# Two of three MLP squares moved to ScalarE, and a planner that keeps a margin ahead of TensorE's attention steps

## The chip, the core and the metric

The kernel runs on one core of one Trainium2 chip. The metric is the device time of one execution in microseconds (us). The median of three runs of the kernel before is 218.18 us (218.15 to 218.87).

## What is computed

Two layers follow each other. The first is a recurrent attention over 4 batches, 8 heads, 768 positions and a head size of 48:

```python
for t in range(S):
    cur = einsum('bhd,bhe->bhde', u[None] * kt, vt)
    y[:, :, t] = einsum('bhd,bhde->bhe', rt, state + cur)
    state = wt[..., None] * state + einsum('bhd,bhe->bhde', kt, vt)
```

The second is an MLP on the 3072 rows of `y` (384 wide, hidden 2048):

```python
h = x @ w_in
r = maximum(h, 0)
out = (s * (r * r) + b) @ w_out
```

## The kernel before, in words

The attention is cut into 24 chunks of 128 positions (6 along the sequence for each of 4 batches; chunk `n` is position block `n // 4` of batch `n % 4`). Within a chunk the recurrence is written as matrix products. A chunk passes these steps, each a small function:

- SyncE issues four loads of 192 KB: `w`, `r`, `k`, `v` (line 212).
- ScalarE takes the logarithm of `w` (`ln`, line 219). TensorE sums it along the chunk (`cum`, lines 268 to 276). ScalarE takes the exponential (`exp`, lines 290 and 294). VectorE multiplies `r` and `k` by it (`mul`, tile `prd`, line 300).
- TensorE transposes the result (`tr`, tile `trps`, line 327), ScalarE copies it out (`tev`, tile `RK`, line 342), TensorE multiplies keys and queries (`mt`, line 352), VectorE masks (`msk`, tile `mt_sb`, line 364), and TensorE forms `y` from the state and the masked scores (`ymm`, lines 380 and 389).
- VectorE adds a diagonal part (`yev`, tile `x_sb`, line 419). That part is made on GpSimd (`rkp`, `rku`, `yd`, lines 224, 235, 255) with a reduction on VectorE between (`cd`, line 249). TensorE transposes again (`xtr`, line 467) and ScalarE copies into the MLP's input `xT` (`xev`, line 482).
- The state is updated by TensorE (`dmm`, line 405), VectorE (`sup`, line 447) and GpSimd (`st`, line 456). `v` is cast to bf16 (`vb`), on GpSimd for the first 8 chunks (line 601) and on ScalarE for the other 16 (line 599), by the string `VBE`.

The MLP works on 12 tiles `T` of 256 rows (two chunks each). A tile has 8 pieces `g1` (6 matmuls of 256 columns each, line 516, into PSUM `h_ps`, 2 buffers). ScalarE applies the ReLU to each (`rh`, line 529) and VectorE squares it (`sq`, tile `gT`, line 534). Then come 8 pieces `g2` (4 matmuls of 384 columns each, line 549, into `o_ps`), four for each half tile, and VectorE scales and adds a constant (`oev`, tile `o_sb`, line 559). The store stands in the same SyncE queue as the loads. The two weights arrive in four pieces each and are cast to bf16: `CIE = 'APAP'` says that `w_in` is cast in turn by ScalarE (A) and GpSimd (P), and `COE = 'ADAD'` that `w_out` is cast by ScalarE and VectorE (D). A sum over `w_out` (`colsum`, line 578) and one ScalarE instruction (`bconst`, line 585) stand before the first `g2`.

The order of the instructions is not that of the loops. A class `Plan` holds each step with its engine, an assumed duration, the steps that it depends on, the buffers that it takes and a priority. It plays the steps through in time by these assumed numbers: again and again the step that can start first is put behind the others of its engine (ties go to the lower priority number). The steps are then written out in that order, and on the chip each engine takes its own in that order and waits where an operand is not there. Attention steps have low priority numbers, MLP pieces on TensorE high ones, so that these fill TensorE's gaps. Steps marked `port=True` (GpSimd's, `mul` and `sq` on VectorE) are planned one at a time.

Before the first 28 us of the plan are over, TensorE's planned gaps are filled with matmuls on a tile of zeros (`warm`, line 757), so many as fit into the gap at 0.125 us each.

Of the kernel before, what the change touches and what calls it, by code (L numbers as in the profile page):

```python
# [10 lines left out]
AF = mybir.ActivationFunctionType  # L11
ALU = mybir.AluOpType
# [4 lines left out]
WIN_AT = 35.0  # L17
WOUT_AT = 45.0
CIE = 'APAP'
COE = 'ADAD'  # L20
VBE = 'P' * 8 + 'A' * 16
WARM = 28.0


class Plan:
# [7 lines left out]
        self.ops = {}  # L33

    def add(self, name, eng, occ, fn, args=(), deps=(), takes=(), prio=0.0,
            lat=0.12, port=False, dma=0.0):
        self.ops[name] = dict(
            name=name, eng=eng, occ=occ, fn=fn, args=args, deps=list(deps),
            takes=list(takes), prio=prio, lat=lat, port=port, dma=dma,
            n=len(self.ops),  # L40
        )

    def order(self):
        ops = self.ops
        end = {}
        free = {}
        port = 0.0
        dma = 0.0
        held = {tag: [] for tag in self.rings}
        queues = {}  # L50
        for o in sorted(ops.values(), key=lambda o: (o["prio"], o["n"])):
            queues.setdefault(o["eng"], []).append(o)
        out = []

        def ready(o):
            t = 0.0
# [12 lines left out]

        while any(queues.values()):  # L70
            best = None
            for eng, q in queues.items():
                e = free.get(eng, 0.0)
                pick = None
                for o in q[: 1 if eng == "SP" else 400]:
                    r = ready(o)
                    if r is None:
# [9 lines left out]
            t, o = best  # L87
# [18 lines left out]
def kernel(  # L106
# [27 lines left out]
    FPQ = 512 // TOK  # L134
    NQ = FT // FPQ
# [104 lines left out]
    def castv(n):  # L240
        c = cb[n]
        vb = work.tile([128, H, D], BF16, name="vb", tag="vb", bufs=6)
        cast(VBE[n], vb, c["v"])
        c["vb"] = vb

    def cdiag(n):
# [280 lines left out]
    def relu(T, i):  # L527
        rh = mlp.tile([128, FPQ, TOK], BF16, name="rh", tag="rh", bufs=4)
        nc.scalar.activation(out=rh, in_=hs[T, i], func=AF.Relu)  # L529
        hs[T, i] = rh  # L530

    def square(T, i):
        rh = hs.pop((T, i))
        nc.vector.tensor_tensor(  # L534
            out=gT[T][:, i * FPQ : (i + 1) * FPQ, :], in0=rh, in1=rh, op=ALU.mult
        )

    os_ = {}

# [82 lines left out]
    for n in range(N):  # L622
        cc, bb = coords(n)
        T, j = divmod(n, CPT)
        keep = cc < NCH - 1
        P = 10.0 * n
        add(("ln", n), "ACT", 0.45, ln, (n,), [("load", n, 0)] + ([("ln", n - 1)] if n else []),
            [("lw", [("cum", n)])], P)
        add(("rkp", n), "POOL", 1.0, pool1, (n,), [("load", n, 1), ("load", n, 2)],
            [("rkp", [("rku", n)])], P, port=True)  # L630
        add(("rku", n), "POOL", 1.0, pool1b, (n,), [("rkp", n), "load_u"],
            [("rku", [("cd", n)])], P, port=True)
        e = CAST[VBE[n]][0]
# [7 lines left out]
        add(("cum", n), "PE", 0.45, cum, (n,), [("ln", n)],  # L641
            [("A", [("exp", n)])], P, lat=0.2)
# [6 lines left out]
        add(("tr", n), "PE", 0.44, trans, (n,), [("mul", n)],  # L649
            [("B", [("tev", n)]), ("RK", [("mt", n), ("ymm", n)])], P - 3, lat=0.2)  # L650
# [6 lines left out]
        add(("ymm", n), "PE", 0.37, ymm, (n,), [("msk", n), ("vb", n)] + prev  # L657
            + ([("sup", n)] if keep else [("supn", n)]),
            [("B", [("yev", n)]), ("x", [("xtr", n)])], P - 6, lat=0.2)
        add(("yev", n), "DVE", 0.48, yevac, (n,), [("ymm", n), ("yd", n)], [], P - 7)  # L660
        add(("xtr", n), "PE", 0.17, xtr, (n,), [("yev", n)],
            [("B", [("xev", n)])], P - 8, lat=0.2)
        add(("xev", n), "ACT", 0.4, xevac, (n,),
            [("xtr", n)] + ([("xev", n - 1)] if j else []),
            [("xT", [("g1", T, NQ - 1)])] if j == 0 else [], P - 8)
        if keep:
            add(("l2", n), "POOL", 0.17, lam2, (n,), [("exp", n)],
                [("l2", [("st", n)])], P - 2, port=True)
            add(("dmm", n), "PE", 0.16, dmm, (n,), [("mul", n), ("vb", n), ("l2", n)] + prev,
                [("B", [("sup", n)])], P - 4, lat=0.2)  # L670
            add(("sup", n), "DVE", 0.48, supd, (n,), [("dmm", n), ("l2", n)] + prev,
                [("stmp", [("st", n)])] if cc else [], P - 5)
            if cc:
                add(("st", n), "POOL", 0.8, sscale, (n,), [("sup", n), ("l2", n)]
                    + [("ymm", n - B)], [], P - 4, port=True)
            else:
                add(("st", n), "DVE", 0.0, lambda n: None, (n,), [("sup", n)], [], P - 5)
        else:
            add(("supn", n), "DVE", 0.0, supd, (n,), [("mul", n)] + prev, [], P - 5)

    BIG = 1000.0
    for T in range(NT):
        P = BIG + 10 * T
        for i in range(NQ):
# [3 lines left out]
                + ([("g1", T, i - 1)] if i else []),  # L688
                [("h", [("relu", T, i)])]
                + ([("gT", [("g2", T, 4 * CPT - 1)])] if i == 0 else []),  # L690
                P, lat=0.2)
            add(("relu", T, i), "ACT", 0.52, relu, (T, i), [("g1", T, i)],
                [("rh", [("sq", T, i)])], -BIG + P)
            add(("sq", T, i), "DVE", 0.35, square, (T, i), [("relu", T, i)],
                [], -BIG + P, port=True)
        for i in range(4 * CPT):
            tt, part = divmod(i, 4)
            need = [("sq", T, ft // FPQ) for ft in range(4 * part, 4 * part + 4)]
# [9 lines left out]
            add(("g2", T, i), "PE", 0.65, g2, (T, i), need, take, P + 1000 + i, lat=0.2)  # L708
# [90 lines left out]
```

## Time and profile before

| | us |
|---|---|
| median of three runs | 218.18 |
| the profiled execution, its own time | 218.39 |
| its span (first to last instruction) | 216.2 |
| TensorE matmuls busy | 194.9 |
| VectorE busy | 158.2 |
| ScalarE busy | 131.0 |
| GpSimd busy | 103.5 |

The time of the profiled execution is 2.2 us longer than its span, which is what lies around the first and the last instruction. The engines are named PE (TensorE; PEld are its weight loads), DVE (VectorE), ACT (ScalarE), POOL (GpSimd) and SPq (SyncE's DMA queue). TensorE's matmuls are pipelined: the time shown for one reaches past the start of the next one, so a busy TensorE isn't necessarily one that takes matmuls as fast as it can.

### The profile page before, as it was taken

The numbers are of one execution on the slowest core, as the hardware profiler recorded it, in microseconds if no ns is written. First come the engines' busy times: TensorE is split into PE (matmuls) and PEld (weight loads), VectorE is DVE, ScalarE is ACT, GpSimd is POOL, SyncE is SP. The second block draws the span as 40 slices with busy tenths as digits, with TensorE's granted clock in tenths as the row PEclk, the third lists the DMA queues.
The fourth block names the chain that finished last, engine by engine and source line by source line (L and its number), as shares of the span: only waits on it lengthen the run. The fifth ranks groups of instructions, "written<-read, shape, count | busy, mean of one in ns | idle before, by whom it ended". The sixth has DMA issues, their size and how long they took to land.

```text
span 216.2 us, 5140 instructions
## 1 busy us (share of the span) xinstructions
PE 194.9 (90%) x2021; PEld 144.0 (67%) x2021; DVE 158.2 (73%) x249; ACT 131.0 (61%) x234; POOL 103.5 (48%) x128
## 2 busy tenths in 40 slices
PE   2999987877999798899998998899799999999993
PEld 1877655655777676677885875677487677777551
DVE  5168779864898979999999799999898344444222
ACT  3146678857398798498983985676465353535100
POOL 2489928307998726594496788288201000000000
PEclk9999999999999999999999999999999999999999
DMA  7999999999999999999999981101000010110022
GB/s 134 175 203 162 352 251 256 377 184 198 174 197 177 191 207 194 211 194 197 205 223 183 200 178 37 39 0 39 36 3 36 36 39 36 38 41 36 36 74 75
DMA packets 107464, 30.42 MB, mean 141 GB/s; under 512 B 100656, under 2 KB 105904, under 8 KB 107440
## 3 DMA queue, kind: packets, MB, share of 16 engines
q1 hardware_dynamic: 107440, 30.09, 69.4%
q8 instruction: 16, 0.26, 0.6%
q14 instruction: 8, 0.07, 0.1%
HBM read 25.36 MB, written 4.72 MB: 139 GB/s over the span
## 4 chain that ended last, share of the span: by engine, by line
PE 44%; DVE 28%; SPq 9%; issue 6%; DMA 5%; ACT 5%; POOL 1%; DVEq 0%; ACTq 0%
PE o_ps L549 15%; PE h_ps L516 13%; SPq L212 9%; DVE gT L534 7%; DVE mt_sb L364 6%; DVE prd L300 5%; PE warm_ps L757 4%; DVE o_sb L559 3%; PE trps L327 3%; DVE x_sb L419 3%; DMA wt<-in_w_dram 2%; DVE cd L249 2%; PE o_psh L549 2%; DMA out_dram<-o_sb 2%; PE mt_ps L352 1%
## 5 line engine op out<-in xcount | busy, mean ns | idle before, releaser
L516 PE MATMUL h_ps<-xT,w_in 128*128 128x256 bf16 x576 | 77.7, 273 | 1.7 <-ACT rh L529 1.3
L529 ACT ACTIVATE rh<-h_ps 128x512 bf16<-128x512 f32 x96 | 57.3, 603 | 30.5 <-PE h_ps L516 29.3
L534 DVE TENSOR_TENSOR gT<-rh 128x512 bf16<-128x512 bf16 x96 | 55.1, 596 | 20.5 <-ACT rh L529 20.5
L549 PE MATMUL o_ps<-w_out,gT 128*128 128x384 bf16 x352 | 69.4, 326 | 0.5 <-DVE o_sb L559 0.2
L516 PEld LDWEIGHTS <-w_in 128*128 128x128 bf16 x576 | 53.0, 98 | 12.8 <-issue 2.2
L549 PEld LDWEIGHTS <-gT 128*128 128x128 bf16 x384 | 36.9, 98 | 19.0 <-issue 1.6
L300 DVE TENSOR_TENSOR prd<-rkt,E 128x768 bf16<-128x768 f32 x24 | 28.1, 1174 | 9.2 <-ACT E L290 9.2
L364 DVE TENSOR_TENSOR mt_sb<-mt_ps,tri_strict 128x1024 bf16<-128x1024 f32 x24 | 29.2, 1216 | 3.0 <-PE mt_ps L352 3.0
L290 ACT ACTIVATE E<-cums 128x768 bf16<-128x768 f32 x24 | 19.5, 812 | 19.3 <-PE cums L276 12.9
L255 POOL TENSOR_TENSOR yd<-vt,cd 128x384 bf16<-128x384 f32 x24 | 21.3, 887 | 19.5 <-DVE cd L249 19.5
L224 POOL TENSOR_TENSOR rkp<-rkt 128x384 f32<-128x384 f32 x24 | 25.4, 1063 | 9.7 <-DMA rkt<-in_k_dram 9.7
L342 ACT COPY RK<-trps 128x1024 bf16<-128x1024 bf16 x24 | 24.4, 1017 | 7.0 <-PE trps L327 6.8
L235 POOL TENSOR_TENSOR rku<-rkp,u_bc 128x384 f32<-128x384 f32 x24 | 25.1, 1048 | 0.2
L456 POOL TENSOR_TENSOR st<-stmp,l 128x384 bf16<-128x384 bf16 x16 | 15.5, 967 | 17.9 <-DVE stmp L447 17.9
L757 PE MATMUL warm_ps<-warm_sb 128*128 128x256 bf16 x109 | 15.6, 295 | 4.0 <-DVE warm_sb L752 4.0
L327 PE MATMUL trps<-identity,prd 128*128 128x128 bf16 x192 | 14.8, 220 | 3.6 <-DVE prd L300 3.6
L219 ACT ACTIVATE logw<-wt 128x384 bf16<-128x384 f32 x24 | 12.7, 531 | 4.8 <-DMA wt<-in_w_dram 4.7
L419 DVE TENSOR_TENSOR x_sb<-y_ps,yd 128x384 bf16<-128x384 f32 x24 | 13.2, 550 | 3.1 <-PE y_ps L389 3.1
L559 DVE SCALAR_TENSOR_TENSOR o_sb<-o_ps,s_bc,bconst 128x384 f32<-128x384 f32 x22 | 13.5, 612 | 2.2 <-PE o_ps L549 2.0
L327 PEld LDWEIGHTS <-prd 128*128 128x128 bf16 x192 | 11.2, 98 | 5.7 <-DVE prd L300 5.1
L757 PEld LDWEIGHTS <-warm_sb 128*128 128x128 bf16 x109 | 11.0, 106 | 5.9 <-DVE warm_sb L752 4.0
L482 ACT COPY xT<-xt_ps 128x384 bf16<-128x384 bf16 x24 | 11.6, 482 | 5.3 <-PE xt_ps L467 5.2
(51 smaller groups left out, 176.8 us busy)
## 6 DMA issues: line engine op xcount, KB each, us to landing
wt<-in_w_dram SPq DMA_DIRECT2D x24, 192.0 KB, 4.4
rkt<-in_r_dram SPq DMA_DIRECT2D x24, 192.0 KB, 4.7
rkt<-in_k_dram SPq DMA_DIRECT2D x24, 192.0 KB, 4.4
vt<-in_v_dram SPq DMA_DIRECT2D x24, 192.0 KB, 4.4
out_dram<-o_sb SPq DMA_DIRECT2D x24, 192.0 KB, 1.9
wi_st<-in_moe_w_in_dram SPq DMA_DIRECT2D x4, 768.0 KB, 8.0
wo_st<-in_moe_w_out_dram SPq DMA_DIRECT2D x4, 768.0 KB, 8.0
u_bc<-in_u_dram SPq DMA_DIRECT2D x1, 192.0 KB, 4.2
```

Of the source, the lines that this page charges most:

```text
L224: nc.gpsimd.tensor_tensor(out=rkp, in0=c["rk"][:, 0].rearrange("t h d -> t (h d)"), in1=c["rk"][:, 1].rearrange("t h d -> t (h d)"), op=AL ...
L235: nc.gpsimd.tensor_tensor(out=rku.rearrange("t h d -> t (h d)"), in0=c["rkp"], in1=u_bc, op=ALU.mult)
L255: nc.gpsimd.tensor_tensor(out=yd, in0=c["v"], in1=c["cd"].unsqueeze(2).to_broadcast([128, H, D]), op=ALU.mult,)
L300: nc.vector.tensor_tensor(out=prd[:, :, :, 0:D].rearrange("t x h d -> t (x h) d"), in0=c["rk"].rearrange("t x h d -> t (x h) d"), in1=c["E ...
L327: nc.tensor.matmul(ps[:, x * HP + p, :], lhsT=c["prd"][:, x, 2 * p : 2 * p + 2, :].rearrange("t h d -> t (h d)"), rhs=identity, is_transpo ...
L342: nc.scalar.copy(out=RK, in_=c["trps"])
L364: nc.vector.tensor_tensor(out=m.rearrange("s g p t -> s (g p) t"), in0=c["mt_ps"].rearrange("s g p t -> s (g p) t"), in1=tri_strict.unsque ...
L516: nc.tensor.matmul(ps[:, f, :], lhsT=w_in_sb[ft // FPP][:, kt, (ft % FPP) * 128 : (ft % FPP + 1) * 128], rhs=xT[T][:, kt, :], start=(f == ...
L529: nc.scalar.activation(out=rh, in_=hs[T, i], func=AF.Relu)
L534: nc.vector.tensor_tensor(out=gT[T][:, i * FPQ : (i + 1) * FPQ, :], in0=rh, in1=rh, op=ALU.mult)
L549: nc.tensor.matmul(ps, lhsT=gT[T][:, ft, tt * 128 : (tt + 1) * 128], rhs=w_out_sb[ft // FPP][:, ft % FPP, :], start=(ft == 0), stop=(ft == ...
L757: nc.tensor.matmul(warm_ps, lhsT=warm_sb[:, 0:128], rhs=warm_sb, start=True, stop=True)
```

## The change

Six things change. The numbers of lines shift by up to 11.

1. From tile `T = 2` on, two of three squares are made by ScalarE, as an activation with the function Square (`sq_eng`, `SQE = 'DAA'`, `SQT = 2`). That is 54 of the 96 squares; VectorE keeps 42.
2. All casts of `v` are on GpSimd (`VBE = 'P'`); 16 leave ScalarE. The two casts of `w_out` that VectorE made are on GpSimd (`COE = 'APAP'`).
3. In the plan, a TensorE step of the attention (from chunk 6 on) may start only `SLACK = 1.0` us after the operands that other engines make for it, and an MLP piece (from `T = 2` on) only `MSL = 0.1` us after them. No wait is added on the chip; what changes is the order.
4. In the plan, a step that follows another of its own engine no longer counts that one's latency.
5. Among steps that could start at the same time, the plan takes the one that could ask for its engine first.
6. A filler of zero matmuls is at most 0.55 times the time from 2.5 us to the step's planned start, which shortens the first filler alone: 7 matmuls stand ahead of the first `cum` where there were 19 (and 22 behind it where there were 23).

```diff
-COE = 'ADAD'
-VBE = 'P' * 8 + 'A' * 16
+COE = 'APAP'
+VBE = 'P'
 WARM = 28.0
+SQE = 'DAA'
+SQT = 2
+MSL = 0.1
+SLACK = 1.0
...
             for d in o["deps"]:
                 if d not in end:
                     return None
-                t = max(t, end[d])
+                own = ops[d]["eng"] == o["eng"]
+                t = max(t, end[d] - ops[d]["lat"] if own else end[d] + o["slack"])
...
                     for d in h[-self.rings[tag]]:
                         if d not in end:
                             return None
-                        t = max(t, end[d])
+                        t = max(t, end[d] + o["slack"])
...
-                    t = max(r, e)
-                    if o["port"]:
-                        t = max(t, port)
+                    ask = max(r, e)
+                    t = max(ask, port) if o["port"] else ask
                     if pick is None or t < pick[0] - 1e-9:
-                        pick = (t, o)
-                if pick and (best is None or pick[0] < best[0]):
+                        pick = (t, ask, o)
+                if pick and (best is None or pick[:2] < best[:2]):
                     best = pick
...
+    def sq_eng(T, i):
+        return "ACT" if SQE[(T * NQ + i) % len(SQE)] == "A" and T >= SQT else "DVE"
+
     def square(T, i):
         rh = hs.pop((T, i))
-        nc.vector.tensor_tensor(
-            out=gT[T][:, i * FPQ : (i + 1) * FPQ, :], in0=rh, in1=rh, op=ALU.mult
-        )
+        g = gT[T][:, i * FPQ : (i + 1) * FPQ, :]
+        if sq_eng(T, i) == "ACT":
+            nc.scalar.activation(out=g, in_=rh, func=AF.Square)
+        else:
+            nc.vector.tensor_tensor(out=g, in0=rh, in1=rh, op=ALU.mult)
...
+        SL = SLACK if n > 5 else 0.0
...
         add(("mt", n), "PE", 0.43, mt, (n,), [("tev", n)],
-            [("A", [("msk", n)])], P - 5, lat=0.2)
+            [("A", [("msk", n)])], P - 5, lat=0.2, slack=SL)
...
-                P, lat=0.2)
+                P, lat=0.2, slack=MSL if T > 1 else 0.0)
...
-            add(("sq", T, i), "DVE", 0.35, square, (T, i), [("relu", T, i)],
-                [], -BIG + P, port=True)
+            e = sq_eng(T, i)
+            add(("sq", T, i), e, 0.35 if e == "DVE" else 0.5, square, (T, i),
+                [("relu", T, i)], [], -BIG + P, port=e == "DVE")
...
-            warm(min(t, WARM) - idle_from - 0.1)
+            warm(min(min(t, WARM) - idle_from - 0.1, 0.55 * (t - 2.5)))
```

`slack=SL` is given in the same way to `cum`, `tr`, `ymm`, `xtr` and `dmm`.

VectorE's queue in the middle of the program, before, around the squares of tile 2 and the `mul` steps (`prd`) of chunks 9 and 10:

```order
L249 TENSOR_REDUCE cd<-rku 128x8 x2
L534 TENSOR_TENSOR gT<-rh 128x512 x4
L300 TENSOR_TENSOR prd_105<-rkt,E 128x16x48
L534 TENSOR_TENSOR gT<-rh 128x512 x2
L300 TENSOR_TENSOR prd_106<-rkt,E 128x16x48
L534 TENSOR_TENSOR gT<-rh 128x512
```

The changed kernel at the squares that tile 2 still has on VectorE (its third and sixth), around the `mul` of chunk 8:

```order
L545 TENSOR_TENSOR gT<-rh 128x512
L423 TENSOR_TENSOR x_sb<-y_ps,yd 128x384
L304 TENSOR_TENSOR prd_107<-rkt,E 128x16x48
L368 TENSOR_TENSOR mt_sb<-mt_ps,tri_strict 128x1024
L253 TENSOR_REDUCE cd<-rku 128x8
L451 TENSOR_TENSOR stmp<-d_ps,st_777 128x384
L545 TENSOR_TENSOR gT<-rh 128x512
```

Where four squares stood in a row ahead of a `prd`, single squares stand between attention steps.

ScalarE's queue, before, at the last ReLUs of tile 2 and the first of tile 3 (`rh`), with a cast of `v`:

```order
L529 ACTIVATE rh_1389<-h_ps_1366 128x512
L529 ACTIVATE rh_1397<-h_ps_1380 128x512
L599 CAST vb_1406<-vt_886 128x384
L219 ACTIVATE logw2_104<-wt_895 128x8x48
L529 ACTIVATE rh_1428<-h_ps_1399 128x512
L342 COPY RK_1430<-trps_1409 128x1024
L529 ACTIVATE rh_1451<-h_ps_1421 128x512
```

And in the changed kernel, from the first ReLU of tile 3 on, with its squares (`gT`):

```order
L533 ACTIVATE rh_1427<-h_ps_1408 128x512
L533 ACTIVATE rh_1447<-h_ps_1420 128x512
L543 ACTIVATE gT_1407<-rh_1447 128x512
L346 COPY RK_1464<-trps_1438 128x1024
L533 ACTIVATE rh_1497<-h_ps_1454 128x512
L543 ACTIVATE gT_1407<-rh_1497 128x512
L533 ACTIVATE rh_1508<-h_ps_1490 128x512
```

The cast of `v` is gone from ScalarE, and behind two of three ReLUs stands the square of the same piece.

TensorE's queue at the last `xtr` (of chunk 23), in the changed kernel; `gT_2824` belongs to tile 8, and its last `g2` piece follows:

```order
L558 MATMUL o_ps_3407<-w_out2_100,gT_2824 128x384
L471 LDWEIGHTS x_sb_3414
L471 MATMUL xt_ps_3425<-identity_85,x_sb_3414 128x128
L471 LDWEIGHTS x_sb_3414
L471 MATMUL xt_ps_3425<-identity_85,x_sb_3414 128x128
L558 LDWEIGHTS gT_2824
L558 MATMUL o_ps_3407<-w_out3_101,gT_2824 128x384
```

And before, where tile 6's `g2` stand ahead (`gT_2376`) and tile 8's `g1` go on behind:

```order
L549 MATMUL o_ps_3169<-w_out0_98,gT_2376 128x384
L467 LDWEIGHTS x_sb_3167
L467 MATMUL xt_ps_3177<-identity_85,x_sb_3167 128x128
L467 LDWEIGHTS x_sb_3167
L467 MATMUL xt_ps_3177<-identity_85,x_sb_3167 128x128
L516 LDWEIGHTS w_in3_97
L516 MATMUL h_ps_3181<-xT_2559,w_in3_97 128x256
```

Counted to the end of the queue, 68 MLP pieces stand behind the last `xtr` before, and 33 in the changed kernel: the attention is spread over more of the program.

More of the change, by code (lines that the diff above doesn't have):

```diff
@@ L35, in add @@
     def add(self, name, eng, occ, fn, args=(), deps=(), takes=(), prio=0.0,
-            lat=0.12, port=False, dma=0.0):
+            lat=0.12, port=False, dma=0.0, slack=0.0):
         self.ops[name] = dict(
@@ L39, in add @@
             takes=list(takes), prio=prio, lat=lat, port=port, dma=dma,
-            n=len(self.ops),
+            slack=slack, n=len(self.ops),
         )
@@ L242, in castv @@
         vb = work.tile([128, H, D], BF16, name="vb", tag="vb", bufs=6)
-        cast(VBE[n], vb, c["v"])
+        cast(VBE[n % len(VBE)], vb, c["v"])
         c["vb"] = vb
@@ L632 @@
             [("rku", [("cd", n)])], P, port=True)
-        e = CAST[VBE[n]][0]
+        e = CAST[VBE[n % len(VBE)]][0]
         add(("vb", n), e, 0.48, castv, (n,), [("load", n, 3)],
@@ L641 @@
         add(("cum", n), "PE", 0.45, cum, (n,), [("ln", n)],
-            [("A", [("exp", n)])], P, lat=0.2)
+            [("A", [("exp", n)])], P, lat=0.2, slack=SL)
         add(("exp", n), "ACT", 0.82, expo, (n,), [("cum", n)],
@@ L649 @@
         add(("tr", n), "PE", 0.44, trans, (n,), [("mul", n)],
-            [("B", [("tev", n)]), ("RK", [("mt", n), ("ymm", n)])], P - 3, lat=0.2)
+            [("B", [("tev", n)]), ("RK", [("mt", n), ("ymm", n)])], P - 3, lat=0.2, slack=SL)
         add(("tev", n), "ACT", 0.92, tevac, (n,), [("tr", n)], [], P - 3)
         add(("mt", n), "PE", 0.43, mt, (n,), [("tev", n)],
-            [("A", [("msk", n)])], P - 5, lat=0.2)
+            [("A", [("msk", n)])], P - 5, lat=0.2, slack=SL)
         add(("msk", n), "DVE", 1.14, mask, (n,), [("mt", n)],
@@ L658 @@
             + ([("sup", n)] if keep else [("supn", n)]),
-            [("B", [("yev", n)]), ("x", [("xtr", n)])], P - 6, lat=0.2)
+            [("B", [("yev", n)]), ("x", [("xtr", n)])], P - 6, lat=0.2, slack=SL)
         add(("yev", n), "DVE", 0.48, yevac, (n,), [("ymm", n), ("yd", n)], [], P - 7)
         add(("xtr", n), "PE", 0.17, xtr, (n,), [("yev", n)],
-            [("B", [("xev", n)])], P - 8, lat=0.2)
+            [("B", [("xev", n)])], P - 8, lat=0.2, slack=SL)
         add(("xev", n), "ACT", 0.4, xevac, (n,),
@@ L707 @@
                 take = [("h" if T == NT - 1 else "o", [("oev", T, tt)])]
-            add(("g2", T, i), "PE", 0.65, g2, (T, i), need, take, P + 1000 + i, lat=0.2)
+            add(("g2", T, i), "PE", 0.65, g2, (T, i), need, take, P + 1000 + i, lat=0.2, slack=MSL if T > 1 else 0.0)
             if part == 3:
```

4 lines of the change are left out of this document (2 added, 2 removed).

## The prediction

> **What bounds the kernel now.** I read the page first, then busy time by stretches, then TensorE's groups of instructions and the chain of waits for the stretch that the first two point at. The page gives the span and each engine's share:
>
> ```profile
> span 216.2 us, 5140 instructions
> PE 194.9 (90%) x2021; PEld 144.0 (67%) x2021; DVE 158.2 (73%) x249; ACT 131.0 (61%) x234; POOL 103.5 (48%) x128
> ```
>
> By stretches (columns: from and to, length, then busy us with counts for PE, PEld, DVE, ACT, POOL, the granted clock of PE, the DMA share, GB/s):
>
> ```profile
> 50.00:170.00 120.00, 112.84 (x1312) 85.00 (x1310) 108.57 (x161) 86.96 (x162) 75.69 (x89) 1.00 0.79 138
> 70.00:80.00 10.00, 8.84 (x98) 7.13 (x94) 8.52 (x15) 8.79 (x19) 4.58 (x7) 1.00 1.12 194
> 80.00:90.00 10.00, 8.50 (x97) 5.97 (x95) 10.00 (x14) 7.07 (x15) 7.58 (x9) 1.00 1.08 208
> 130.00:140.00 10.00, 8.38 (x86) 6.00 (x84) 9.48 (x14) 5.90 (x10) 5.73 (x7) 1.00 0.11 41
> 150.00:160.00 10.00, 8.46 (x93) 5.97 (x92) 9.04 (x14) 4.88 (x7) 2.84 (x3) 1.00 0.11 39
> 170.00:180.00 10.00, 9.95 (x77) 7.33 (x75) 4.14 (x10) 4.78 (x8) 0.00 (x0) 1.00 0.12 41
> ```
>
> From 170 on only MLP work is left and TensorE is full. Between 50 and 170, where attention and MLP mix, it is idle for 120 - 112.84 = 7.16 us, and four of the twelve windows hold 1.16 + 1.50 + 1.62 + 1.54 = 5.82 of that. VectorE is at 108.6 of 120 there, the fullest engine beside TensorE.
>
> Busy TensorE time hides short waits, so I count slots instead. The chain of waits has back-to-back matmuls, 12 of 256 columns in 1.31 us, which is 0.109 us each or 0.4264 ns a column; the first four lines are from the stretch 70 to 80:
>
> ```profile
> 70.83 0.63 DVE gT L534
> 71.50 1.72 DVE gT L534 x3
> 73.23 1.69 DVE prd L300
> 74.96 0.64 PE trps L327 x8
> ...
> 175.16 1.31 PE h_ps L516 x12
> ```
>
> TensorE's groups in 50 to 170 give the columns:
>
> ```profile
> L516 PE MATMUL h_ps<-xT,w_in 128*128 128x256 bf16 x341 | 46.5, 273 | 0.0
> L549 PE MATMUL o_ps<-w_out,gT 128*128 128x384 bf16 x224 | 43.9, 326 | 0.2 <-DVE o_sb L559 0.2
> L327 PE MATMUL trps<-identity,prd 128*128 128x128 bf16 x152 | 11.7, 220 | 2.9 <-DVE prd L300 2.9
> L352 PE MATMUL mt_ps<-RK 48*128 48x128 bf16 x152 | 7.5, 219 | 0.0
> L389 PE MATMUL y_ps<-vb,mt_sb 128*128 128x48 bf16 x152 | 6.9, 183 | 0.0
> L380 PE MATMUL y_ps<-st,RK 128*128 128x96 bf16 x76 | 6.3, 206 | 0.0
> L467 PE MATMUL xt_ps<-identity,x_sb 128*128 128x128 bf16 x57 | 6.3, 220 | 1.5 <-DVE x_sb L419 1.5
> L271 PE MATMUL cums<-logw,ntri_incl 128*128 128x384 bf16 x19 | 6.2, 325 | 0.0
> L268 PE MATMUL cums<-logw,tri_strict 128*128 128x384 bf16 x19 | 6.2, 325 | 1.1 <-ACT logw L219 1.1
> L405 PE MATMUL d_ps<-vb,prd 128*128 128x96 bf16 x60 | 5.1, 207 | 2.5 <-DVE prd L300 2.4
> ```
>
> Counts by columns: 87,296 + 86,016 + 19,456 + 19,456 + 7,296 + 7,296 + 7,296 + 7,296 + 7,296 + 5,760 = 254,464 columns, 108.5 us. So the stretch loses 120 - 108.5 = **11.5 us** of TensorE time: 7.2 visible as idle, 4.3 hidden, since a matmul shown as 273 ns holds its slot for only 109 and covers a wait of up to 0.16. The releasers named are VectorE's `prd` and `x_sb`. In the chain, four squares stand in VectorE's queue ahead of a `prd`, TensorE's `trps` waits for that, and every MLP piece behind `trps` waits too. That 11.5 us is what the change can win here.
>
> **Squares and casts.** The durations (stretch 50 to 170, then VectorE from 170 on, then ScalarE's casts, GpSimd's casts and VectorE's cast of the whole program):
>
> ```profile
> L534 DVE TENSOR_TENSOR gT<-rh 128x512 bf16<-128x512 bf16 x56 | 35.2, 658 | 2.1 <-ACT rh L529 2.1
> L529 ACT ACTIVATE rh<-h_ps 128x512 bf16<-128x512 f32 x56 | 33.8, 605 | 11.0 <-PE h_ps L516 10.0 <-DVE x_sb L419 0.4 <-DVE mt_sb L364 0.2
> L534 DVE TENSOR_TENSOR gT<-rh 128x512 bf16<-128x512 bf16 x24 | 10.2, 426 | 17.6 <-ACT rh L529 17.6
> L599 ACT CAST vb<-vt 128x384 bf16<-128x384 f32 x16 | 8.3, 519 | 0.3 <-DMA vt<-in_v_dram 0.3
> L599 ACT CAST w_out<-wo_st 128x1536 bf16<-128x1536 f32 x2 | 2.9, 1473 | 0.1
> L601 POOL CAST vb<-vt 128x384 bf16<-128x384 f32 x8 | 4.7, 591 | 0.3 <-DMA vt<-in_v_dram 0.3
> L601 POOL CAST w_in<-wi_st 128x1536 bf16<-128x1536 f32 x2 | 3.0, 1503 | 4.0 <-DMA wi_st<-in_moe_w_in_dram 4.0
> L603 DVE CAST w_out<-wo_st 128x1536 bf16<-128x1536 f32 x2 | 1.9, 954 | 0.7 <-DMA wo_st<-in_moe_w_out_dram 0.7
> ```
>
> Of the 54 squares that move, 38 lie in this stretch (tiles 2 to 8), 16 in the last one. The same square takes VectorE 658 ns here and 426 ns from 170 on, where GpSimd is silent. VectorE sheds 38 x 0.658 = 25.0 us: 108.6 falls to 83.6.
>
> The trace has no Square on ScalarE. From below, a cast of 384 elements from SBUF takes it 519 ns, from above one of 1536 takes 1473; the line between them is 0.828 ns an element and gives 0.62 us for 512. The ReLU of the same shape, from PSUM, takes 0.605. I take 0.62, with ends of 0.52 and 0.9 (0.9 is near the middle between the two casts). ScalarE gains 38 x 0.62 = 23.6 and loses 16 x 0.519 = 8.3: 87.0 becomes 102.3. GpSimd gains 16 x 0.591 = 9.5 and goes from 75.7 to 85.2, all covered by its own idle time; its casts can hold VectorE's remaining squares up, but VectorE then has 25 us to spare.
>
> [...]
>
> **Where the 11.5 us goes.** TensorE's own work is the same. The eight better windows have 7.16 - 5.82 = 1.34 us of idle in 80, 0.17 per 10 us. Were the four bad ones like them, visible idle would remain at that rate; the hidden part is 4.3 / 12 = 0.36 per 10 us. A margin of 1.0 us in the plan, and 0.1 for MLP pieces, covers waits of the hidden size, so I let a quarter of them stand: 0.17 + 0.09 = 0.26 per 10 us, over about 111 us 2.9. The ends: 0.17 (1.9 us) and 0.53 (5.9 us). **Gain 8.6 us, between 5.6 and 9.6.** The margin itself puts no wait on the chip; it lets `g1` and `g2` pieces of 0.65 us stand ahead of an attention step that would have been late. What it costs is that a chunk comes out later, the second rival.
>
> **The front.** These rows of the timeline stand between the weights and the first `g2`, and the two lines ahead of them are the first filler and the first `w_in` cast:
>
> ```profile
> 3.98 3.96 PE L757 MATMUL warm_ps<-warm_sb 128*128 128x256 bf16 x19 [3.98 <-DVE warm_sb L752]
> 24.36 1.47 ACT L599 CAST w_in<-wi_st 128x1536 bf16<-128x1536 f32 x1
> ...
> 45.86 2.76 PE L578 MATMUL cs_ps<-w_out,ones 128*128 128x384 bf16 x16
> 46.01 0.96 DVE L603 CAST w_out<-wo_st 128x1536 bf16<-128x1536 f32 x1 [0.71 <-DMA wo_st<-in_moe_w_out_dram]
> 50.13 0.97 PE L549 MATMUL o_ps<-w_out,gT 128*128 128x384 bf16 x5
> ```
>
> Twelve fillers fewer let the first `cum` start up to 12 x 3.96 / 19 = 2.5 us earlier, but the first `g1` stands behind the `w_in` cast at 24.36, whose weights come through a load queue whose order doesn't change there: nothing reaches the end. The last `w_out` cast becomes 1.50 us where it was 0.95, ending at 47.5. The last four of the 16 `colsum` matmuls need it, and they run from about 48 now, so the 0.55 is just hidden, and costs 0.5 if `colsum` comes earlier. Between `colsum`'s end (48.6) and the first `g2` (50.1) 1.5 us go by with `bconst` and a `cum` behind it; if the first three quarters of `colsum` come earlier, up to 1.3 of it goes. I take +0.4 gained, ends -0.5 and +1.3. Stores move past loads in SyncE's queue, at no cost: in the whole stretch ScalarE's `ln` waits 1.4 us for loads:
>
> ```profile
> ACT logw L219 <- DMA wt<-in_w_dram: 1.4, 2, 0.7
> ```
>
> **The end.** From 170 on ScalarE and VectorE are half idle; 16 squares on either cost nothing.
>
> The sum is made against the profiled execution, 218.39 us (span 216.2 and 2.2 around it, 0.2 above the median of the three runs): 218.4 - 8.6 - 0.4 = **209.4 us**. The forecast's own ends: 218.4 - 9.6 - 1.3 = 207.5 and 218.4 - 5.6 + 0.5 = 213.3.
>
> **Rivals.**
>
> *ScalarE takes VectorE's place (slower).* In the stretch ScalarE then has 78.7 + 38p us of work, p being the price of a square. VectorE loses TensorE 11.5 us at 108.6; ScalarE reaches 108.6 at p = 0.79, and from there the time is 218 again plus 38 us for each further us of p: p = 0.9 gives 218.4 - 0.4 + 38 x 0.11 = 222. For it: at p = 0.62 ScalarE is at 102 of 111, no emptier than VectorE was, and ScalarE stands in every chunk's path four times (`ln`, `exp`, `tev`, `xev`). Against: the nearest rows give 0.6. [...] Chance 0.05.
>
> *The attention comes out too late (slower).* Behind the last `xtr` 33 MLP pieces are left, 33 x 0.654 = 21.6 us, where 68 were. For 209.4 that `xtr` must stand at about 209.4 - 2.2 - 4.3 - 21.6 = 181 (4.3 is from the last matmul to the span's end). Now the last `xT` copy is at 167, and chunks follow each other by (167 - 58) / 18 = 6.1 us; 181 allows 6.8. Five margins of 1 us in a chunk's chain, with one PSUM buffer for `cum` and `mt` in turn, could make it more; at 7.3 us a chunk the `xtr` is at 190, and the time is 218 again, at 7.6 it is 224. Against: chunks overlap, and nothing on the chip waits for the margin. Rows of the ends:
>
> ```profile
> 58.33 0.48 ACT L482 COPY xT<-xt_ps 128x384 bf16<-128x384 bf16 x1 [2.13 <-PE xt_ps L467]
> 167.16 0.48 ACT L482 COPY xT<-xt_ps 128x384 bf16<-128x384 bf16 x1 [0.22 <-PE xt_ps L467]
> 211.91 0.63 DVE o_sb L559
> ```
>
> Chance 0.05.
>
> *The waits only change their name.* VectorE's backlog goes, but the plan's numbers still miss ScalarE's, and half of the 11.5 stays: 218.4 - 5.7 + 1 = 213.7. Chance 0.10.
>
> *It does nothing*: the losses come from the order, not from VectorE, and the new order loses as much. 218.0. Against it, the named releasers. Chance 0.02.
>
> **How the numbers follow.** The forecast has 0.78, the rivals 0.05, 0.05, 0.10 and 0.02. A measurement of this kernel tells about 0.5% (1.1 us) from no change. Faster by more: 0.78 + 0.10 = 0.88. Same: 0.02. Slower: 0.10. The range is the forecast's own, 207.5, up to the third rival's 213.7; the two slower cases and the last, 0.12, are left out.
>
> **What would show it.** In the profile after: Square on ScalarE near 0.62 us; VectorE's remaining squares well under 0.658; TensorE idle under 0.3 per 10 us from 50 to 160; the last attention step near 181; the first `g2` at 49 to 50. The forecast is wrong if Square takes over 0.75, if TensorE waits on ScalarE's `RK`, `xT` or `gT` where it waited on `prd`, or if the `g1` of tile 11 waits for the last `xT`.

## The result and the profile after

The changed kernel takes **210.89 us** (median; 210.61 to 210.94), beside 218.17 us for the kernel before on the same chip (217.55 to 218.87). The ratio is 0.966 (95% interval 0.963 to 0.969): 7.3 us faster. The profiled execution took 210.94 us, 7.45 less than the one before. Two disturbed executions are left out of the medians of the experiments: one of 1093 us with the squares moved alone, and one of 244.25 us with all squares on ScalarE. The page after, its span and the engines' shares:

```profile
span 209.0 us, 5056 instructions
PE 192.6 (92%) x2008; PEld 143.8 (69%) x2008; DVE 126.3 (60%) x193; ACT 151.7 (73%) x272; POOL 117.7 (56%) x146
```

The same stretches as before (from and to, length, busy us with counts for PE, PEld, DVE, ACT, POOL, granted clock, DMA share, GB/s):

```profile
50.00:170.00 120.00, 118.28 (x1313) 89.79 (x1312) 81.35 (x122) 101.66 (x188) 86.09 (x105) 0.99 0.77 141
70.00:80.00 10.00, 9.46 (x119) 7.39 (x117) 7.14 (x12) 9.21 (x18) 8.48 (x11) 1.00 1.02 182
80.00:90.00 10.00, 9.76 (x108) 7.25 (x106) 7.34 (x12) 9.22 (x19) 8.91 (x12) 1.00 1.08 209
130.00:140.00 10.00, 9.76 (x113) 7.70 (x112) 6.79 (x11) 8.91 (x19) 8.29 (x10) 1.00 0.07 25
150.00:160.00 10.00, 9.99 (x100) 7.07 (x100) 5.04 (x8) 9.08 (x17) 0.00 (x0) 1.00 0.05 20
```

TensorE's idle time in the stretch fell from 7.16 to 1.72 us, and the four bad windows, which had 5.82 of it, have 1.03. VectorE went from 108.6 to 81.4, ScalarE from 87.0 to 101.7, GpSimd from 75.7 to 86.1; forecast were 83.6, 102.3 and 85.2. At the place where four squares stood ahead of a `prd` in the chain of waits, `trps` now follows other matmuls without a gap:

```profile
76.04 1.42 PE h_ps L520 x12
77.46 0.17 PE d_ps L409 x4
77.63 0.45 PE trps L331 x8
78.08 0.65 PE h_ps L520 x6
```

What TensorE's matmuls wait for in the stretch (us in total, times, longest), first the longest entries of the kernel before (the list has 1.1 us for `logw` besides, which lie ahead of 50, and 0.2 for `o_sb`):

```profile
PE trps L327 <- DVE prd L300: 2.9, 3, 1.5
PE d_ps L405 <- DVE prd L300: 2.4, 2, 1.6
PE xt_ps L467 <- DVE x_sb L419: 1.5, 3, 0.8
```

and this is all that it lists after:

```profile
PE o_ps L558 <- DVE o_sb L568: 1.1, 2, 0.5
PE h_ps L520 <- ACT xT L486: 0.5, 2, 0.2
```

No wait for `prd` or `x_sb` is left. TensorE's groups of instructions in the stretch give the columns, as before:

```profile
L520 PE MATMUL h_ps<-xT,w_in 128*128 128x256 bf16 x384 | 51.0, 273 | 0.5 <-ACT xT L486 0.5
L558 PE MATMUL o_ps<-w_out,gT 128*128 128x384 bf16 x252 | 49.0, 332 | 1.2 <-DVE o_sb L568 1.1
L331 PE MATMUL trps<-identity,prd 128*128 128x128 bf16 x136 | 10.4, 219 | 0.0
L356 PE MATMUL mt_ps<-RK 48*128 48x128 bf16 x136 | 6.8, 219 | 0.0
L393 PE MATMUL y_ps<-vb,mt_sb 128*128 128x48 bf16 x136 | 6.2, 183 | 0.0
L384 PE MATMUL y_ps<-st,RK 128*128 128x96 bf16 x68 | 5.7, 206 | 0.0
L471 PE MATMUL xt_ps<-identity,x_sb 128*128 128x128 bf16 x51 | 5.6, 219 | 0.0
L275 PE MATMUL cums<-logw,ntri_incl 128*128 128x384 bf16 x17 | 5.5, 324 | 0.0
L272 PE MATMUL cums<-logw,tri_strict 128*128 128x384 bf16 x17 | 5.5, 323 | 0.0
L409 PE MATMUL d_ps<-vb,prd 128*128 128x96 bf16 x60 | 5.0, 206 | 0.0
```

98,304 + 96,768 + 17,408 + 17,408 + 6,528 + 6,528 + 6,528 + 6,528 + 6,528 + 5,760 = 268,288 columns, 13,824 more than before in the same 120 us. At 0.4264 ns a column that is 114.4 us of work, so 5.6 us are lost where 11.5 were: 1.7 visible as idle time, 3.9 in matmul time beyond the columns' slots. That second part is called hidden here, as in the prediction; what is in it is taken up below.

The first `g2` and the two instructions it waits for, from the timeline after (start, us, engine, line, operation, count, and in brackets the idle time ahead of it):

```profile
45.77 1.46 POOL L610 CAST w_out<-wo_st 128x1536 bf16<-128x1536 f32 x1 [2.11 <-DMA wo_st<-in_moe_w_out_dram]
47.29 0.81 PE L587 MATMUL cs_ps<-w_out,ones 128*128 128x384 bf16 x4 [1.63 <-POOL w_out L610]
48.77 4.37 PE L558 MATMUL o_ps<-w_out,gT 128*128 128x384 bf16 x16 [0.27 <-ACT bconst L594]
```

The first `g2` starts 1.36 us earlier than before, but its 16 matmuls take 4.37 us, where 16 x 384 columns at 0.4264 ns are 2.6. The clock says why (stretches as above):

```profile
44.00:47.00 3.00, 1.25 (x7) 0.54 (x6) 2.23 (x4) 2.67 (x5) 1.23 (x1) 1.00 0.82 153
...
48.00:49.00 1.00, 0.73 (x8) 0.41 (x7) 0.00 (x0) 0.86 (x2) 0.92 (x1) 0.83 1.15 230
...
50.00:51.00 1.00, 1.00 (x5) 0.49 (x4) 0.82 (x2) 0.52 (x1) 0.78 (x3) 0.50 1.26 210
...
52.00:53.00 1.00, 1.00 (x8) 0.58 (x7) 0.00 (x0) 0.00 (x0) 0.85 (x3) 0.96 1.40 189
```

In this execution TensorE was busy 1.25 of 3 us from 44 to 47, and from about 48.7 to 52.1 its granted clock was 0.50 (0.83 in the window from 48 is 0.34 us at 0.50, and 0.96 in that from 52 is 0.08).

The last attention step (`xtr`) and the last result, also from the timeline:

```profile
183.09 0.33 PE L471 MATMUL xt_ps<-identity,x_sb 128*128 128x128 bf16 x3
205.03 0.62 DVE L568 SCALAR_TENSOR_TENSOR o_sb<-o_psh,s_bc,bconst 128x384 f32<-128x384 f32 x1 [1.98 <-PE o_psh L558]
```

### The profile page after: what moved, and what is told of

It reads as the page before. It is cut to its first block, busy times and chain, and to the rows that moved or that the text cites. A ratio compares the mean times of both kernels' runs of the same rounds, so it can differ in the third digit from the quotient of the medians.

```text
span 209.0 us, 5056 instructions
## 1 busy us (share of the span) xinstructions
PE 192.6 (92%) x2008; PEld 143.8 (69%) x2008; DVE 126.3 (60%) x193; ACT 151.7 (73%) x272; POOL 117.7 (56%) x146
## 4 chain that ended last, share of the span: by engine, by line
PE 73%; DMA 11%; SPq 9%; DVE 2%; ACT 1%; issue 1%; POOL 1%; ACTq 0%
PE o_ps L558 28%; PE h_ps L520 26%; SPq L216 7%; DMA wo_st<-in_moe_w_out_dram 6%; DMA wt<-in_w_dram 5%; PE trps L331 4%; PE mt_ps L356 3%; PE o_psh L558 2%; PE y_ps L393 2%; PE y_ps L384 1%; PE cums L272 1%; PE cums L275 1%; PE xt_ps L471 1%; SPq L491 1%; PE d_ps L409 1%; DVE o_sb L568 1%
## 5 line engine op out<-in xcount | busy, mean ns | idle before, releaser
L520 PE MATMUL h_ps<-xT,w_in 128*128 128x256 bf16 x576 | 75.4, 273 | 2.8 <-ACT w_in L608 1.3
L558 PE MATMUL o_ps<-w_out,gT 128*128 128x384 bf16 x352 | 67.6, 332 | 1.5 <-DVE o_sb L568 1.1
L533 ACT ACTIVATE rh<-h_ps 128x512 bf16<-128x512 f32 x96 | 56.0, 595 | 11.2 <-PE h_ps L520 11.0
L543 ACT ACTIVATE gT<-rh 128x512 bf16<-128x512 bf16 x54 | 34.0, 630 | 1.7
L304 DVE TENSOR_TENSOR prd<-rkt,E 128x768 bf16<-128x768 f32 x24 | 24.2, 1008 | 14.3 <-ACT E L294 13.2
L545 DVE TENSOR_TENSOR gT<-rh 128x512 bf16<-128x512 bf16 x42 | 24.4, 593 | 12.7 <-ACT rh L533 12.6
L228 POOL TENSOR_TENSOR rkp<-rkt 128x384 f32<-128x384 f32 x24 | 24.1, 1005 | 5.6 <-DMA rkt<-in_k_dram 5.4
L318 POOL TENSOR_TENSOR l<-lam,par 128x8 f32<-128x8 f32 x20 | 15.7, 787 | 5.6 <-ACT lam L298 5.2
L768 PE MATMUL warm_ps<-warm_sb 128*128 128x256 bf16 x96 | 13.9, 293 | 4.0 <-DVE warm_sb L763 4.0
L253 DVE TENSOR_REDUCE cd<-rku 128x8 f32<-128x384 f32 x24 | 13.1, 546 | 6.0 <-POOL rku L239 5.9
```

Source lines behind the costliest of these rows:

```text
L228: nc.gpsimd.tensor_tensor(out=rkp, in0=c["rk"][:, 0].rearrange("t h d -> t (h d)"), in1=c["rk"][:, 1].rearrange("t h d -> t (h d)"), op=AL ...
L304: nc.vector.tensor_tensor(out=prd[:, :, :, 0:D].rearrange("t x h d -> t (x h) d"), in0=c["rk"].rearrange("t x h d -> t (x h) d"), in1=c["E ...
L520: nc.tensor.matmul(ps[:, f, :], lhsT=w_in_sb[ft // FPP][:, kt, (ft % FPP) * 128 : (ft % FPP + 1) * 128], rhs=xT[T][:, kt, :], start=(f == ...
L543: nc.scalar.activation(out=g, in_=rh, func=AF.Square)
L545: nc.vector.tensor_tensor(out=g, in0=rh, in1=rh, op=ALU.mult)
L558: nc.tensor.matmul(ps, lhsT=gT[T][:, ft, tt * 128 : (tt + 1) * 128], rhs=w_out_sb[ft // FPP][:, ft % FPP, :], start=(ft == 0), stop=(ft == ...
```

## The experiments

**The theory**: VectorE takes its instructions in order, squares stood ahead of `prd` (four of them from 70.83 us on, the `prd` at 73.23, in the chain of waits before) and `x_sb`, and every MLP piece behind the late attention step waited too; taking squares away from that queue wins most, the margin and the casts of `v` the rest. **The main rival**: the new order (margin, rules of the planner) won, and where the squares are made matters little. Each ratio is to the kernel before timed beside it, whose medians were 218.91 us (for the first four experiments), 218.11 (the next four) and 218.33. The diffs are against the changed kernel where nothing else is said. Where an edit changes what the plan knows (engines, margins), the plan makes a new order, so that more differs on the chip than the edited steps; the order stays only with the zeros, with the long filler, and in the three kernels in which squares are left out or made twice.

| kernel | us | ratio to before (95%) | TensorE idle in 50 to 170 |
|---|---|---|---|
| before | 218.17 | 1 | 7.2 |
| after | 210.89 | 0.966 (0.963 to 0.969) | 1.7 |
| squares back on VectorE | 226.54 | 1.037 (1.031 to 1.042) | 10.3 |
| before, squares moved alone | 213.76 | 0.979 (0.973 to 0.984) | 2.3 |
| the planner's part alone | 222.12 | 1.015 (1.008 to 1.022) | 8.0 |
| casts of `v` back on ScalarE | 216.34 | 0.990 (0.985 to 0.995) | 6.3 |
| no margins | 214.98 | 0.985 (0.982 to 0.988) | 5.3 |
| all squares from tile 2 on ScalarE | 238.77 | 1.097 (1.092 to 1.101) | 15.7 |
| zeros in `colsum`'s gap | 210.31 | 0.965 (0.962 to 0.967) | 2.5 |
| first filler long | 210.27 | 0.965 (0.962 to 0.968) | 2.4 |
| before's order, squares left out | 212.37 | 0.972 (0.970 to 0.974) | 2.7 |
| after's order, VectorE loaded | 217.66 | 0.997 (0.993 to 1.000) | 7.7 |
| after's order, ScalarE loaded | 230.04 | 1.054 (1.052 to 1.055) | 13.7 |
| smaller margins, zeros | 209.49 | 0.959 (0.957 to 0.960) | 1.2 |

The last column is 120 minus TensorE's busy time in the stretch. It is time in one profiled execution, and in slower kernels work runs on past 170.

### Squares back on VectorE

```diff
-SQE = 'DAA'
+SQE = 'D'
```

> All squares are on VectorE again; casts, margins, the plan's rules and the filler stay as changed. Theory (VectorE's load between 50 and 170 is what cost TensorE its time): VectorE gets back 38 squares of 0.66 us, 25 us, and has more GpSimd work beside it than before the change, so at least the old loss comes back: 218 to 223 us. Rival (the margin in the order wins the time): most of the 7.3 us stays won, below 214 us.

Measured 226.5 us, slower than the kernel before and than the theory's number; the rival is refuted. VectorE wasn't fuller than it had been before, though:

```profile
50.00:170.00 120.00, 109.66 (x1155) 81.08 (x1154) 91.41 (x144) 67.95 (x126) 84.34 (x105) 0.94 0.79 141
100.00:110.00 10.00, 6.73 (x93) 5.01 (x91) 7.21 (x11) 3.79 (x6) 9.92 (x13) 0.73 1.19 187
```

VectorE is at 91.4 of 120 and TensorE's clock at 0.94, at 0.73 in one window. The timelines of ScalarE and VectorE show where it starts: the `exp` of a chunk is done at 67.0, and the `mul` that reads it runs at 91.3, behind squares; for one of these VectorE stands idle 5.0 us.

```profile
66.21 0.83 ACT L294 ACTIVATE E<-cums 128x768 bf16<-128x768 f32 x1
...
91.30 1.58 DVE L304 TENSOR_TENSOR prd<-rkt,E 128x768 bf16<-128x768 f32 x1
```

So the order in this place, not a full VectorE, holds the attention up there: the time is in the theory's direction, its reason isn't what the trace shows. How much of the whole loss this place and the lower clock make was not tried apart.

### Squares moved alone, planner and casts as before

Against the kernel before, the hunks of `sq_eng` and `square`, and the one by which the plan counts these squares as ScalarE's (not shown); the plan's rules are those of before:

```diff
+SQE = 'DAA'
+SQT = 2
...
+        if sq_eng(T, i) == "ACT":
+            nc.scalar.activation(out=g, in_=rh, func=AF.Square)
```

> The kernel before, with nothing but two of three squares moved to ScalarE from tile 2 on. Theory: most of the gain is there without margin, casts or filler, 5 to 7 of the 7.3 us: 211 to 213.5 us. Rival (margin): under a third of it, over 215.5 us.

Measured 213.8 us: just outside the theory's interval, well under the rival's. The ratio gives 2.15% or 4.7 us (3.5 to 5.9 by its interval), about two thirds of the whole gain.

```profile
50.00:170.00 120.00, 117.68 (x1327) 89.12 (x1327) 85.82 (x122) 106.24 (x208) 79.98 (x89) 1.00 0.80 140
```

ScalarE is fuller here (106.2) than VectorE is, and TensorE's idle time is 2.3 us all the same.

### The planner's part alone

Squares and casts as in the kernel before, everything else as changed:

```diff
-COE = 'APAP'
-VBE = 'P'
+COE = 'ADAD'
+VBE = 'P' * 8 + 'A' * 16
-SQE = 'DAA'
+SQE = 'D'
```

> The margins, the plan's other rules and the short filler, with squares and casts on the engines that they had before. Theory: an order with a margin can't win TensorE time while VectorE is full, and chunks come out later: 217 to 221 us. Rival (margin): 211 to 214 us.

Measured 222.1 us, 1.5% slower than before and above the interval. Alone, margin, planner's rules and short filler lose 3.2 us (1.7 to 4.7). VectorE was busy 93.4 of 120 us there, so the theory's reason, a full VectorE, isn't what this trace shows either.

### Casts of `v` back on ScalarE

```diff
-VBE = 'P'
+VBE = 'P' * 8 + 'A' * 16
```

> The changed kernel with the casts of v of chunks 8 to 23 back on ScalarE (16 of 0.52 us). Theory of the first rival of the prediction (ScalarE is now nearly as full as VectorE was): ScalarE goes from 101.7 to about 110 us of work in 50 to 170, at the level at which VectorE lost TensorE 11.5 us: 214 to 218 us. Rival (ScalarE has room, the casts matter little): 210.5 to 212 us.

Measured 216.3 us: 5.4 us of the gain hang on where 16 casts of half a microsecond stand, with the order that the plan makes of it.

```profile
50.00:170.00 120.00, 113.69 (x1281) 86.06 (x1280) 83.29 (x119) 106.08 (x202) 77.60 (x89) 1.00 0.76 140
```

ScalarE is no fuller (106.1) than with the squares moved alone (106.2), where TensorE lost 2.3 us; here it is idle for 6.3. So the share of busy time isn't the reason. The order differs from that kernel's by the margins, the plan's other rules, the filler and two casts of `w_out`; which of these costs the 4 us was not tried.

### No margins

```diff
-MSL = 0.1
-SLACK = 1.0
+MSL = 0.0
+SLACK = 0.0
```

> The changed kernel with SLACK = 0 and MSL = 0; squares, casts, the plan's other rules and the filler stay. Theory (the margin is worth something once VectorE and ScalarE have room, though it cost 1.5% alone): 213 to 215.5 us. Rival (the margin only costs, squares and casts win all): 208 to 210.5 us.

Measured 215.0 us, as expected: with squares and casts moved, the margins are worth 4.1 us.

### All squares from tile 2 on ScalarE

```diff
-SQE = 'DAA'
+SQE = 'A'
```

> The changed kernel with all squares from tile 2 on made by ScalarE (SQE = 'A'). Theory (the engine that has most work beside TensorE sets the loss, and ScalarE is next): 18 more squares of 0.63 us in tiles 2 to 8 take ScalarE from 101.7 to 113 us of work for what are now 120 us, more than VectorE had before: slower than before the change, 220 to 228 us. Rival (TensorE's order alone decides, ScalarE has room): 210 to 214 us.

The direction was right, the size far off: 238.8 us.

```profile
50.00:170.00 120.00, 104.28 (x1084) 74.33 (x1083) 62.96 (x89) 89.88 (x165) 82.07 (x101) 1.00 0.76 140
```

ScalarE is at 89.9 of 120, less than in the changed kernel, and VectorE at 63. No engine is full, and TensorE is idle for 15.7 us. Two of the longer entries in the list of waits from 50 to 200:

```profile
ACT RK L346 <- PE trps L331: 22.0, 8, 3.6
PEld L558 <- ACT gT L543: 9.5, 11, 1.0
```

TensorE's `g2` weight loads wait for ScalarE's squares, and ScalarE stands 22 us behind `trps`, which TensorE has late: the two in-order queues seem to wait for each other in turn. TensorE's matmuls wait 6.6 us for VectorE's `o_sb` besides. That this is the whole cause is not shown.

### The front: zeros in `colsum`'s gap, and the long first filler

The first keeps TensorE busy with matmuls on zeros, which add nothing to the sum; the second takes the sixth part of the change back.

```diff
+            for _ in range({8: 3, 12: 9}.get(ft, 0)):
+                nc.tensor.matmul(ps, lhsT=warm_sb[:, 0:128],
+                    rhs=w_out_sb[0][:, 0, :], start=False, stop=False)
```

```diff
-            warm(min(min(t, WARM) - idle_from - 0.1, 0.55 * (t - 2.5)))
+            warm(min(t, WARM) - idle_from - 0.1)
```

> The changed kernel with 12 matmuls of zeros added into the colsum sum while it waits for the last w_out pieces, so that TensorE is not idle from 45.7 to 47.3 us and the granted clock should stay at 1.00 where it was 0.50 from 48.2 to 52. Theory (until about 60 the first attention chunk after the weights, chunk 5, sets the time, so the 1.8 us lost at half clock were not on the path): 210.2 to 211.0 us. Rival (TensorE is the bound from its first g2 on): 208.8 to 209.5 us.

> The changed kernel with the first filler as before (19 matmuls). Theory (the first 24 us wait for the weights' loads): no difference beyond 0.5 us, 210.4 to 211.4 us. Rival (what the first chunk wins, 2.5 us, arrives at the end in part): 212 to 213.4 us.

With zeros the clock is full where it had been 0.50:

```profile
50.00:51.00 1.00, 1.00 (x8) 0.52 (x6) 1.00 (x2) 0.46 (x1) 0.78 (x2) 1.00 1.14 205
```

The time is 210.3 us, as the theory had it. With the long filler it is 210.3, 0.1 under what was expected. The intervals of both overlap with that of the change, and the medians are 0.6 us apart: neither the half clock nor the filler's length makes a difference that these runs resolve.

That the zeros kept the clock full is not shown. With the long filler, and no zeros, it was 1.00 in these windows too, and so it was without margins, though TensorE did less in the gap than in the changed kernel:

```profile
44.00:47.00 3.00, 0.82 (x5) 0.38 (x4) 0.88 (x3) 1.91 (x5) 1.46 (x1) 1.00 0.75 134
```

The four executions of the changed kernel itself differ: mean granted clocks of 1.00, 0.997, 0.992 and 0.990 go with 210.61, 210.89, 210.94 and 210.90 us. By these the half clock seems to cost about 0.3 us at the end, in those executions that have it.

### Before's order, squares left out

The kernel before with nothing moved, but for the 54 squares, which are left out: the ReLU writes their part of `gT` itself, so the MLP's result lacks the square there.

```diff
     def relu(T, i):
+        if left_out(T, i):
+            rh = gT[T][:, i * FPQ : (i + 1) * FPQ, :]
...
+        if left_out(T, i):
+            return
```

> The kernel before in its own order; two of three squares from tile 2 on are left out (the ReLU writes into gT itself), so that the result is not squared there. Nothing moves and ScalarE gets nothing more. Theory (what VectorE has in its queue ahead of the attention steps is what costs TensorE): VectorE loses 25 us in 50 to 170 and the time falls by most of the 11.5 us, to 208 to 212 us. Rival (the order is what costs, whatever VectorE has to do): over 215.5 us.

Measured 212.4 us, a little above the theory's interval, far under the rival's: with every other instruction in its old place, emptying VectorE's queue alone wins 6.0 us. A left-out square also makes its `gT` ready earlier and frees `rh`, but nothing speaks for that as the gain: the list of waits of the kernel before has none for `gT` in the stretch, of TensorE or of ScalarE.

```profile
50.00:170.00 120.00, 117.35 (x1351) 89.80 (x1350) 91.00 (x125) 87.53 (x166) 76.99 (x89) 1.00 0.76 140
```

### After's order, with VectorE or ScalarE loaded

Every square that ScalarE makes is made a second time, into a tile that nobody reads, by VectorE in the one and by ScalarE in the other:

```diff
             nc.scalar.activation(out=g, in_=rh, func=AF.Square)
+            nc.vector.tensor_tensor(out=g2nd, in0=rh, in1=rh, op=ALU.mult)
```

```diff
             nc.scalar.activation(out=g, in_=rh, func=AF.Square)
+            nc.scalar.activation(out=g2nd, in_=rh, func=AF.Square)
```

> The changed kernel in its own order; each square that ScalarE makes is made a second time on VectorE, into a tile that nobody reads. Theory (VectorE's load): VectorE gets about 22 us back in 50 to 170, from 81 to 103 us, and time is lost though no step that anyone waits for has moved: 214 to 219 us. Rival (the new order with its margin carries the gain): under 212.5 us.

> The changed kernel in its own order; each square that ScalarE makes is made a second time on ScalarE, into a tile that nobody reads: the price of a square goes from 0.63 to about 1.2 us. First rival of the prediction (78.7 + 38 x p us of work on ScalarE, slower than before from p = 0.8 on): 222 to 236 us. Against it (ScalarE has slack at the places that count): under 218 us.

VectorE loaded: 217.7 us, as expected. 6.8 of the 7.3 us are lost again with nothing moved. TensorE's matmuls wait for VectorE at several places, 3.0 us for `o_sb`, 1.1 for `mt_sb`, 0.5 for `prd`, and one of the old waits is back:

```profile
50.00:170.00 120.00, 112.26 (x1221) 82.83 (x1219) 106.29 (x154) 94.22 (x175) 90.16 (x105) 0.99 0.78 141
```

```profile
PE xt_ps L471 <- DVE x_sb L423: 2.4, 3, 1.2
```

ScalarE loaded: 230.0 us, as expected. A square then costs ScalarE 0.630 + 0.613 = 1.24 us, and TensorE waits for the ReLU:

```profile
L543 ACT ACTIVATE gT<-rh 128x512 bf16<-128x512 bf16 x37 | 23.3, 630 | 1.2
L545 ACT ACTIVATE g2nd<-rh 128x512 bf16<-128x512 bf16 x37 | 22.7, 613 | 0.0
```

```profile
PE h_ps L520 <- ACT rh L533: 7.7, 15, 0.7
```

### Smaller margins and zeros

```diff
-MSL = 0.1
-SLACK = 1.0
+MSL = 0.3
+SLACK = 0.4
```

and the zeros as above.

> The changed kernel with SLACK = 0.4 and MSL = 0.3 in the place of 1.0 and 0.1, and with the zeros in the colsum sum as in the run e7. Theory (what the margin must cover is the 0.1 to 0.4 us by which the plan misses a step, for the MLP pieces too, and a smaller margin lets the chunks out earlier): 209 to 210.3 us. Rival (the values at hand are the best for this order): 210.5 to 212.5 us.

Measured 209.5 us (208.75 to 209.52), as expected: 4.1% faster than before, and its interval lies below that of the changed kernel.

The zeros alone gave 0.965, so most of the step to 0.959 seems to be the margins; they were not run without the zeros.

## Why the prediction was right, and the step that was off

**The bound** was read rightly. The 11.5 us of lost TensorE time were the place of the gain: 5.9 us of the 7.45 are columns that TensorE now does in the stretch and didn't before (13,824 x 0.4264 ns). That VectorE's queue was the cause is shown from both sides with no instruction moved: squares left out won 6.0 us, VectorE loaded lost 6.8.

**The prices** held. The groups of the stretch after:

```profile
L543 ACT ACTIVATE gT<-rh 128x512 bf16<-128x512 bf16 x42 | 26.5, 630 | 1.3
L545 DVE TENSOR_TENSOR gT<-rh 128x512 bf16<-128x512 bf16 x21 | 10.7, 511 | 6.7 <-ACT rh L533 6.7
```

Square on ScalarE takes 0.630 us where 0.62 was taken, from the line between two casts; VectorE's remaining squares fell from 0.658 to 0.511. Of the first, 42 lie in the stretch and not 38, since more MLP work fits into it.

**The size of the stretch's gain was off**: 5.9 us, where 8.6 was forecast with ends of 5.6 and 9.6. The visible part came out better than the better windows had been (1.72 / 12 = 0.14 per 10 us, where 0.17 was taken). The step that failed is the hidden part, 4.3 us taken as waits that matmuls cover, of which "I let a quarter of them stand". Measured are 3.9, of which the half clock is 1.0. About half of the 4.3 was no wait: the count by columns leaves out what small matmuls take. The rows of one-column matmuls, which the lists of columns leave out, first of the kernel before, then after:

```profile
L276 PE MATMUL cums<-ones,logw 128*128 128x1 bf16 x60 | 3.6, 164 | 0.0
L280 PE MATMUL cums<-ones,logw 128*128 128x1 bf16 x56 | 3.4, 164 | 0.0
```

And from the chain of waits after, at a place where nothing is waited for:

```profile
86.79 0.20 PE y_ps L393 x8
...
87.32 0.08 PE cums L280 x4
87.40 1.32 PE o_ps L558 x8
```

Four matmuls of one column take 0.08 us or a little more (0.10 from 53.92 to 54.02 in the timeline after), where their columns count as nothing, and eight of 48 columns take 0.20, where 0.16 is counted. By an estimate from these lines that is 15 x 0.09 + 19 x 0.04 = 2.1 us in the stretch before and 14 x 0.09 + 17 x 0.04 = 1.9 after, which no margin can win. The hidden waits proper fell from about 2.2 us to about 1.0. With that the prediction's own steps would have given about 7 us and not 8.6. Adding the half clock's 1.0 to the 5.9 would close the rest, but the two executions with full clock don't bear it out: with zeros and with the long filler the stretch loses 5.9 and 5.7 us, counted in the same way, 2.5 and 2.4 of them visible.

**The front** gave about nothing, where 0.4 was forecast: 1.36 us at the first `g2`, at the upper end of +1.3, and 1.8 lost again at half clock in this execution. At full clock, with the zeros, TensorE stands idle for 0.9 us between 50 and 60, where it was 0.15, 0.4 of it for `prd` and 0.3 for `mt_sb`: the attention steps right behind are late. **Around the ends** 0.55 us came that no step had: the time outside the span fell from 2.2 to 1.9, and that behind the last `o_sb`'s start from 4.3 to 4.0. The other 0.9 or so, up to 7.45, is work done ahead of 50 and behind 170. That the total lies within 1.5 us of the forecast is in part luck: the stretch gave 2.7 us less than forecast, and the rest of the program about 1.1 us more.

**The parts don't add up.** The forecast costed the planner's part by what it covers. Alone it is worth -3.2 us, beside the other two +4.1; the squares alone +4.7; the casts, taken back alone, 5.4. An order planned with margins seems to be as good as the planned durations of its fullest queues (the plan takes 0.35 us for a square on VectorE, which took 0.658 before): with all squares on VectorE, the `mul` at 91.3 shows what the plan put behind them. Planned durations were not varied.

**The rivals.** *ScalarE takes VectorE's place*: its price of 0.79 was not reached. With 1.24 a square, its rule gives 218.4 - 0.4 + 38 x 0.45 = 235, and the kernel with ScalarE loaded took 230. But the idea under it, that the busy share of the fullest engine sets the loss, fell: all squares on ScalarE took 238.8 us at 89.9 of 120. Which engine makes a square doesn't decide alone either: 54 squares moved alone to ScalarE gained 4.7 us (a square takes 0.630 us there in the changed kernel, and took VectorE 0.658 before), though all 80 of tiles 2 to 11 there, beside the change's other parts, lost 21. *The attention comes out too late*: the last `xtr` is at 183.1, two us behind the forecast's 181 and seven ahead of the 190 from which this rival decides, and from there to 203 TensorE is busy without a gap. (At 7.6 us a chunk this rival's own sum gives 223, not 224.) *The waits only change their name*: it had half of the 11.5 us stay, and counted by slots 5.6 do, nearer to this rival than to the forecast's 2.9. But 1.9 of these are no waits and 1.0 is half clock, and the waits that have a name are 1.1 us for VectorE's `o_sb` and 0.5 for ScalarE's `xT`. A wait on `xT` is one of the prediction's signs of being wrong; at 0.5 us it decides nothing. Its time, 213.7, is 2.8 us too long. *It does nothing* was refuted by the result.

## What to carry to other kernels

Ask of a full in-order engine what stands in its queue ahead of the steps that the bottleneck waits for: here 6 us hung on squares that nobody was in a hurry for. Busy shares rank suspects, but they did not tell a good order from a bad one (ScalarE busy 90 of 120 us took 239 us, 106 took 214), so after each move the order has to be tuned again, margins included. When waits are counted as slots, take first what small matmuls need from a piece of the chain without waits: here half of what was taken for hidden waits was their own time.

## What the hardware showed

- In the profiled execution of the changed kernel TensorE's granted clock was 0.50 for 3.4 us, behind a stretch in which it was busy for 1.25 of 3 us; since its first matmul it had never been idle for more than 1.63 us at a time. The clock need not fall there: TensorE busy for 0.82 of the same 3 us, in the kernel without margins, kept 1.00. What decides between the two is not shown here. The half clock cost 1.8 us where it happened and, by the changed kernel's executions (one at full clock against three), about 0.3 at the end.
- The same 128 x 512 square took VectorE 426 ns with GpSimd silent (from 170 on, before), 658 and 511 ns in the stretch before and after, where GpSimd works for part of it (75.7 and 86.1 of 120 us), and with VectorE loaded 704 (GpSimd 90.2):

```profile
L545 DVE TENSOR_TENSOR g2nd<-rh 128x512 bf16<-128x512 bf16 x38 | 26.7, 704 | 2.0 <-ACT rh L533 1.7
```
